# Weight conversion in half steps, one every fourth attention slot, ahead of the row maximum

## The chip, the cores and the metric

The kernel runs on one core of one Trainium2 chip. The metric is the device time of one launch in microseconds (us). Lower is better. The engines are TensorE (PE in the profile; its weight loads are PEld), VectorE (DVE), ScalarE (ACT), GpSimd (POOL) and SyncE (SP), which here only issues transfers. Each takes its instructions in the order in which they stand in its queue; PE may load weights ahead.

## The reference

```python
def _attn_ref(q, k, v, centroids):          # q, k, v: 2 x 8 x 768 x 64, centroids: 8 x 16 x 64
    q_assign = np.argmax(np.einsum('bhsd,hcd->bhsc', q_n, c_n), axis=-1)   # q_n, k_n, c_n: normalized rows
    k_assign = np.argmax(np.einsum('bhsd,hcd->bhsc', k_n, c_n), axis=-1)
    mask = q_assign[:, :, :, None] == k_assign[:, :, None, :]
    scores = np.where(mask, scale * np.matmul(q, k.transpose(0, 1, 3, 2)), -1e9)
    attn = softmax(scores)
    return np.matmul(attn, v)

x = attn_out.transpose(0, 2, 1, 3).reshape(1536, 512)
h = x @ moe_w_in;  x = (h * np.cos(h)) @ moe_w_out        # 512 -> 2048 -> 512, first mixture
h = x @ moe2_w_in; g = blend(h)                           # second mixture: 0, (h+1)^2/4 or h
return g @ moe2_w_out
```

The four weight matrices come as 64-bit floats, which the chip's engines don't multiply.

## The kernel before

**Attention.** The 16 heads are done in 8 pairs of heads, and each pair in 24 slots (one `run_slot` each), 192 slots in all. A slot transposes one 384-column block of the softmax numerator (`p_transpose`: three PE transposes `pt`, an ACT copy `phi`, a DVE remainder `plo`), computes half a score tile (`scores`, two matmuls into `s`) and multiplies earlier blocks with v (`p_v`, into `o`). Every second slot has a row maximum (`row_max`, line 484, DVE, result `nm`) and the exponential that needs it (`row_exp`, ACT). `later(n, f)` puts work n slots ahead. On slots 18 to 179 the order on PE, ACT, DVE and POOL is the order in which the code is written; SP's order and the rest are a scheduler's.

**The next pair's preparation** (`prep_pair`) goes along, a piece a slot: transposes of q and k, their split into two parts `th` and `tl` on POOL (lines 301, 302), the cluster masks, `vv` (lines 439, 440), and copies of `th`, `tl` into the stacked operands `st` by SP transfers (line 315). There are three buffers for `st`. The copies into the second head of pair 5 can start only when the scores of pair 4's first head, the last of which stands in slot 99, have read the buffer. For pairs 1, 3 and 5 `th` and `tl` lie in one buffer of `w0pool`, tag `w_0` (line 282; the trace calls the tile `t`).

**POOL's other work** is the finish of each block of 384 rows: `o_rows` (`xt`, lines 567 and 568), whose sum DVE multiplies with the transposed denominators (`finish`, line 579), and `x_parts` (`xh`, `xl`, lines 584, 585); and the denominators (`den`, `rb`, lines 502, 513).

**Weights.** The 16 tiles of 512x512 come in 32 chunks of 128x1024 64-bit words. `convert_chunk` makes float32 out of one in six steps: ACT takes an absolute value (line 139), DVE clips (141), shifts (143), puts low bits in (146) and the sign and POOL rounds to the first part (149, 155; then the next chunk's load is issued), DVE computes the second part (158). `pump(n)` does the next n steps. `wx` and `wraw`, the chunk and its raw words, have one buffer each. The first tile of weights is written into `w_0`, the buffer that pair 5's `th` and `tl` leave; it can be written first when all their readers are done: the matmuls and all ten copies. In the attention there are 16 steps, one every eighth slot from 69 to 189, behind the slot's row maximum.

**Mixtures.** Per quarter of the hidden width and block of 512 tokens `hidden` makes four groups of 12 matmuls into `h`, each with DVE and ACT work to `gh`, `gl`, and `output` four into `y`. Each group pumps one step. `weight` pumps what is still missing of a tile before its first use. The first two `hidden` calls come ahead of the first `output`.

Of the kernel before, what the change touches and what calls it, by code (L numbers as in the profile page):

```python
# [8 lines left out]
F32 = mybir.dt.float32  # L9
F32R = mybir.dt.float32r  # L10
I32 = mybir.dt.int32
BF16 = mybir.dt.bfloat16
I64 = mybir.dt.int64
AF = mybir.ActivationFunctionType
ALU = mybir.AluOpType
# [3 lines left out]
P = 128  # L19
# [3 lines left out]

HIGH_MIN = 2.0 ** -15
HIGH_MAX = 122876.0
CHUNK = 6
P_BUFS = 6
NDVE = 2
NIDLE = (9, 3, 5, 7, 6)
# [3 lines left out]
def attention_moe_moe(  # L33
# [18 lines left out]
    nc = tc.nc  # L52
# [8 lines left out]
    NQ = DFF // 512  # L61
# [44 lines left out]
    def next_slot():  # L106
        now[0] += 1
        for f, args in due.pop(now[0], ()):
            f(*args)
# [9 lines left out]
    w0pool = ctx.enter_context(tc.tile_pool(name="w0pool", bufs=1))  # L119
    wslot = []  # L120
    wchunks = []
    wraw = {}

    def issue_chunk(n):
        if n >= len(wchunks):
            return
        src, c0, _ = wchunks[n]
        raw = w0pool.tile([P, 2, 512], I64, tag="wraw", bufs=1, name=f"wraw{n}")
        nc.sync.dma_start(raw, src[:, c0:c0 + 2])
        wraw[n] = raw  # L130

    def convert_chunk(n):

        _, c0, w = wchunks[n]
        words = wraw.pop(n).bitcast(I32).rearrange("p c (f t) -> p c f t", t=2)
        low, high = words[:, :, :, 0], words[:, :, :, 1]
        x = w0pool.tile([P, 2, 512], F32, tag="wx", bufs=1, name=f"wx{n}")
        xi = x.bitcast(I32)
        nc.scalar.activation(x, high.bitcast(F32), AF.Abs)  # L139
        yield  # L140
        nc.vector.tensor_scalar(x, x, HIGH_MIN, HIGH_MAX, ALU.max, ALU.min)
        yield
        nc.vector.tensor_scalar(xi, xi, 3, 0x3FFFFFFF,
                                ALU.logical_shift_left, ALU.bitwise_and)
        yield
        nc.vector.scalar_tensor_tensor(xi, low, 29, xi,
                                       ALU.logical_shift_right, ALU.bitwise_or)
        yield
        nc.vector.scalar_tensor_tensor(xi, high, -0x40000000, xi,
                                       ALU.bitwise_and, ALU.bitwise_or)  # L150
        if not wslot:
            wslot.append(w0pool.tile([P, 2, 4, 512], F32R, tag="w_0", name="w_0"))
        t = wslot[w % 4]
        hi, lo = t[:, 0, c0:c0 + 2], t[:, 1, c0:c0 + 2]
        nc.gpsimd.tensor_scalar(hi, x, 1.0, 0.0, ALU.mult, ALU.add)  # L155
        issue_chunk(n + 1)
        yield
        nc.vector.tensor_tensor(lo, x, hi.bitcast(F32), ALU.subtract)
        yield

    for l, (wi, wo) in enumerate(((w1_in, w1_out), (w2_in, w2_out))):
        for qi in range(NQ):
# [6 lines left out]
    def weight_steps():  # L169
        for n in range(len(wchunks)):  # L170
            for _ in convert_chunk(n):
                yield n
# [3 lines left out]
    def pump(n):  # L176

        for _ in range(n):
            at[0] += 1
            next(wsteps, None)  # L180

    at = [0]

    def weight(l, qi, s):
        pump(2 * CHUNK * ((l * NQ + qi) * 2 + s + 1) - at[0])
        t = wslot[((l * NQ + qi) * 2 + s) % len(wslot)]
        return t[:, 0], t[:, 1]


    with ExitStack() as actx:  # L190
# [273 lines left out]
        def scores(n, step):  # L464

            i, h, hf = units[n // HJ]
            j = hf * HJ + n % HJ
            qt, kt = prepped[i][1][h]
            if step == 0:
                ptile[n] = ps_s.tile([P, 2, 512], F32, tag="s", name=f"s{n}")  # L470
            s = ptile[n]
            cols = slice(j * P, (j + 1) * P)
            kc = slice(step * HS, (step + 1) * HS)
            with tc.issue_after(last_po[0]) if n == 0 and step == 0 else ExitStack():
                nc.tensor.matmul(s[:, step, :HS], qt[:, 0, cols], kt[:, 0, kc],  # L475
                                 start=True, stop=False)
            rows = D + C if i else D + 2 * C
            nc.tensor.matmul(s[:, step, :HS], qt[:rows, 1, cols], kt[:rows, 1, kc],  # L478
                             start=False, stop=True)

        def row_max(n):
            nm = ap.tile([P, 1], F32, tag="nm", bufs=8, name=f"nm{n}")
            s = ptile[n]
            nc.vector.tensor_reduce(nm, s[:, :, :HS], AX.XY, ALU.max, negate=True)  # L484
            ptile[n] = (s, nm)

        def row_exp(n):
            s, nm = ptile[n]
# [34 lines left out]
        def p_transpose(u, kt):  # L523
            ps = ps_t.tile([P, HS], F32, tag="t", name=f"pt{u}_{kt}")
            for jj in range(HJ):
                p = ptile[u * HJ + jj].rearrange("p a n -> p (a n)")
                nc.tensor.transpose(ps[:, jj * P:(jj + 1) * P], p[:, kt * P:(kt + 1) * P], ident)  # L527
            hi = ap.tile([P, HS], F32R, tag="phi", bufs=6, name=f"phi{u}_{kt}")
            lo = ap.tile([P, HS], F32R, tag="plo", bufs=6, name=f"plo{u}_{kt}")
            nc.scalar.activation(hi, ps, AF.Copy)  # L530
            pts[(u, kt)] = (hi, lo, ps)

        def p_lo(u, kt):
            hi, lo, ps = pts[(u, kt)]
            nc.vector.tensor_tensor(lo, ps, hi.bitcast(F32), ALU.subtract)  # L535

        def p_v(u, kt):
            i, h, hf = units[u]
            vv = prepped[i][0]
            hi, lo, _ = pts.pop((u, kt))  # L540
            if kt == 0:
                opsum[u] = ps_o.tile([P, HS], F32, tag="o", name=f"o{u}")
            o = opsum[u]
            lhs = vv[:, kt, h * P:(h + 1) * P]
            nc.tensor.matmul(o, lhs, hi, start=(kt == 0), stop=False)  # L545
            nc.tensor.matmul(o, lhs, lo, start=False, stop=(kt == NJ - 1))  # L546
            if kt == NJ - 1:
                later(1, o_parts, u)
# [61 lines left out]
        def run_slot(slot):  # L610
            g = slot + LEAD
            if slot in prep_at:
                preps.append(prep_pair(prep_at[slot]))
            if 0 <= slot < NSLOT:
                p_transpose(slot // NJ, slot % NJ)
            if 0 <= g < NSLOT:
                scores(g // 2, g % 2)
            for u, kt in pv_slots.get(slot, ()):
                p_v(u, kt)
            if slot % 2 == 0:  # L620
                for s in (slot - 1, slot):
                    if 0 <= s < NSLOT:
                        p_lo(s // NJ, s % NJ)
                if 2 <= g < NSLOT + 2:
                    row_exp(g // 2 - 1)
            next_slot()
            if slot == 60:
                issue_chunk(0)
            preps[:] = [p for p in preps if next(p, 0) != 0]
            if slot % 2 == 1 and 0 <= g < NSLOT:  # L630
                row_max(g // 2)
            if 64 <= slot < 192 and slot % 8 == 5:
                pump(1)

# [61 lines left out]
    def mm3(o, lh, ll, rh, rl, first, last):  # L698
        nc.tensor.matmul(o, lh, rh, start=first, stop=False)  # L699
        nc.tensor.matmul(o, lh, rl, start=False, stop=False)  # L700
        nc.tensor.matmul(o, ll, rh, start=False, stop=last)  # L701

    def hidden(l, qi, blk):
        wh, wl = weight(l, qi, 0)
        gh = mp.tile([P, 4, BW], F32R, tag="gh", bufs=2, name=f"gh{l}_{qi}_{blk}")
        gl = mp.tile([P, 4, BW], F32R, tag="gl", bufs=2, name=f"gl{l}_{qi}_{blk}")
        cols = slice(blk * BW, (blk + 1) * BW)
        for f in range(4):
            next_slot()
            ph = ps_h.tile([P, BW], F32, tag="h", name=f"h{l}_{qi}_{blk}_{f}")  # L710
            fs = slice(f * P, (f + 1) * P)
            for c in range(4):
                mm3(ph, wh[:, c, fs], wl[:, c, fs], xh[:, c, cols], xl[:, c, cols],
                    c == 0, c == 3)
            (g_cosine if l == 0 else g_blend)(ph, gh[:, f], gl[:, f], f"{l}_{qi}_{blk}_{f}")
            pump(1)
        return gh, gl

    def output(l, qi, blk, gh, gl):
# [69 lines left out]
```

## Time and profile before

| | |
|---|---|
| runs | 815.85, 817.35, 819.4 us; median 817.35 |
| profiled execution | 820.39 us, of which the span from first to last instruction is 818.6 |
| PE busy | 797.4 us, 97% of the span |
| DVE busy | 629.7 us, 77% |
| ACT busy | 400.3 us, 49% |
| POOL busy | 282.6 us, 35% |
| mean granted TensorE clock | 0.991 of full speed |

Busy time is the time in which an engine works on an instruction; a PE that waits inside a chain of small matmuls can still look busy, since their ends are modelled and overlap. The attention ends near 283 us; what follows is the two mixtures. Times in the views below are from the start of the span. A bracket in a row of a timeline gives the idle time of the engine just before it and whose work ended it.

### The profile page before, as it was taken

The page shows a single profiled execution, that of the slowest core. Times are in us where ns is not written, and L with a number is a line of the kernel's source. Part 1 is how long each engine was busy: PE and PEld are TensorE (multiplying, and loading weights), DVE is VectorE, ACT ScalarE, POOL GpSimd, SP SyncE. Part 2 cuts the span into 40 slices and gives each one's busy share as a digit, 9 for nine tenths or more (in the row PEclk, how much of TensorE's full clock was granted, in tenths as well). Part 3 has the DMA queues.
Part 4 walks back from the last instruction along what each step waited for, and adds up shares of the span by engine and source line. Part 5 has one row for each costly group of instructions (what it writes and reads, how often), then busy time and mean ns, then how long its engine had stood idle before and what let it go on. Part 6 is the DMA issues. An engine that isn't in the chain of part 4 may idle for free.

```text
span 818.6 us, 11285 instructions
## 1 busy us (share of the span) xinstructions
PE 797.4 (97%) x4042; PEld 670.6 (82%) x4042; DVE 629.7 (77%) x957; ACT 400.3 (49%) x762; POOL 282.6 (35%) x425
## 2 busy tenths in 40 slices
PE   8899999999999999999999999999999999999998
PEld 5789988889888877888888888888888888888886
DVE  6878978968899787777977777898876987755552
ACT  3688878767788665443434333323444233222220
POOL 3347558574674532222221112332231122111110
PEclk9999999988999999999999999999999999999999
DMA  7875553565440103213121313112122221000012
GB/s 155 192 147 121 134 126 88 119 154 108 97 89 32 52 2 103 92 63 103 52 91 64 102 52 104 52 54 100 52 70 86 61 86 59 1 1 0 14 50 91
DMA packets 48183, 65.97 MB, mean 81 GB/s; under 512 B 27904, under 2 KB 32640, under 8 KB 48128
## 3 DMA queue, kind: packets, MB, share of 16 engines
q1 hardware_dynamic: 47984, 65.22, 29.5%
q8 instruction: 32, 0.52, 0.3%
q14 instruction: 23, 0.19, 0.1%
q10 hardware_dynamic: 144, 0.03, 0.0%
HBM read 43.02 MB, written 3.15 MB: 56 GB/s over the span
## 4 chain that ended last, share of the span: by engine, by line
PE 76%; DVE 10%; POOL 6%; ACT 4%; issue 2%; DMA 1%; SPq 0%; POOLq 0%; ACTq 0%; DVEq 0%
PE y L699 11%; PE y L700 11%; PE y L701 11%; PE h L701 10%; PE h L699 10%; PE h L700 10%; PE pt L527 4%; DVE plo L535 3%; DVE nm L484 3%; PE s L475 2%; PE s L478 2%; PE o L546 2%; PE o L545 2%; ACT phi L530 1%; PE pd L368 1%
## 5 line engine op out<-in xcount | busy, mean ns | idle before, releaser
L657 POOL TENSOR_SCALAR gh<-g 128x512 fp32r<-128x512 f32 x96 | 71.5, 745 | 278.0 <-DVE g L688 157.4
L699 PE MATMUL h<-xh,w 128*128 128x512 f32 x384 | 151.4, 394 | 0.5 <-DVE g L674 0.5
L700 PE MATMUL h<-xl,w 128*128 128x512 f32 x384 | 151.4, 394 | 0.0
L701 PE MATMUL h<-xh,w 128*128 128x512 f32 x384 | 151.3, 394 | 0.0
L535 DVE TENSOR_TENSOR plo<-pt,phi 128x384 fp32r<-128x384 f32 x192 | 99.6, 547 | 16.6 <-ACT phi L530 15.8
L530 ACT ACTIVATE phi<-pt 128x384 fp32r<-128x384 f32 x192 | 93.2, 494 | 36.2 <-PE pt L527 34.4
L484 DVE TENSOR_REDUCE nm<-s 128x1 f32<-128x768 f32 x96 | 91.0, 948 | 19.8 <-PE s L478 18.8
L527 PE MATMUL pt<-ident,p 128*128 128x128 f32 x576 | 98.5, 279 | 7.8 <-DVE plo L535 5.8
L684 ACT ACTIVATE p<-h,mone 128x512 f32<-128x512 f32 x48 | 33.1, 690 | 130.0 <-DVE m L683 129.6
L493 ACT ACTIVATE p<-s,nm 128x768 f32<-128x768 f32 x96 | 86.6, 902 | 8.8 <-DVE nm L484 7.8
L661 DVE TENSOR_TENSOR gl<-g,gh 128x512 fp32r<-128x512 f32 x96 | 71.6, 746 | 20.0 <-POOL gh L657 15.3
L699 PEld LDWEIGHTS h<-xh,w 128*128 128x128 f32 x384 | 71.9, 187 | 18.4 <-DVE g L674 1.0
L701 PEld LDWEIGHTS h<-xh,w 128*128 128x128 f32 x384 | 71.8, 187 | 17.7
L527 PEld LDWEIGHTS pt<-ident,p 128*128 128x128 f32 x576 | 69.9, 141 | 20.0 <-issue 4.2
L700 PEld LDWEIGHTS h<-xl,w 128*128 128x128 f32 x384 | 71.9, 187 | 17.5
L475 PE MATMUL s<-st,st 128*128 128x384 f32 x192 | 81.6, 425 | 2.5 <-ACT p L493 2.3
L139 ACT ACTIVATE wx<-wraw 128x1024 f32<-128x1024 f32 x32 | 36.5, 1140 | 95.5 <-DMA wraw<-in_moe_w_out_dram 47.7
L699 PE MATMUL y<-gh,w 128*128 128x512 f32 x192 | 74.9, 390 | 1.3 <-POOL w L155 1.3
L700 PE MATMUL y<-gl,w 128*128 128x512 f32 x192 | 74.8, 390 | 0.0
L700 PE MATMUL y<-w,gh 128*128 128x512 f32 x192 | 74.8, 390 | 0.0
L699 PE MATMUL y<-w,gh 128*128 128x512 f32 x192 | 74.7, 389 | 0.0
L738 DVE TENSOR_TENSOR acc<-y,acc 128x512 f32<-128x512 f32 x72 | 49.2, 685 | 33.1 <-PE y L701 33.1
(120 smaller groups left out, 1636.3 us busy)
## 6 DMA issues: line engine op xcount, KB each, us to landing
wraw<-in_moe_w_in_dram SPq DMA_DIRECT2D x16, 1024.0 KB, 5.1
wraw<-in_moe_w_out_dram SPq DMA_DIRECT2D x16, 1024.0 KB, 4.9
st<-t SPq DMA_DIRECT2D x24, 192.0 KB, 4.3
st<-th SPq DMA_DIRECT2D x9, 384.0 KB, 4.0
st<-tl SPq DMA_DIRECT2D x18, 192.0 KB, 4.0
st<-th SPq DMA_DIRECT2D x18, 192.0 KB, 4.3
nat<-in_q_dram SPq DMA_DIRECT2D x8, 384.0 KB, 5.1
nat<-in_k_dram SPq DMA_DIRECT2D x8, 384.0 KB, 5.8
```

The source lines that it names most:

```text
L475: nc.tensor.matmul(s[:, step, :HS], qt[:, 0, cols], kt[:, 0, kc], start=True, stop=False)
L484: nc.vector.tensor_reduce(nm, s[:, :, :HS], AX.XY, ALU.max, negate=True)
L493: nc.scalar.activation(p, s[:, :, :HS], AF.Exp, bias=nm, accum_out=dens[u][:, jj, 0:1])
L527: nc.tensor.transpose(ps[:, jj * P:(jj + 1) * P], p[:, kt * P:(kt + 1) * P], ident)
L530: nc.scalar.activation(hi, ps, AF.Copy)
L535: nc.vector.tensor_tensor(lo, ps, hi.bitcast(F32), ALU.subtract)
L657: nc.gpsimd.tensor_scalar(hi, g, 1.0, 0.0, ALU.mult, ALU.add)
L661: nc.vector.tensor_tensor(lo, g, hi.bitcast(F32), ALU.subtract)
L699: nc.tensor.matmul(o, lh, rh, start=first, stop=False)
L700: nc.tensor.matmul(o, lh, rl, start=False, stop=False)
L701: nc.tensor.matmul(o, ll, rh, start=False, stop=last)
L738: nc.vector.tensor_tensor(a, po, a, ALU.add)
```

## The change

Each of the first three chunks is converted in halves of 128x512: every step is two steps, first on one half, then on the other, twelve in all. In the attention one such step is done every fourth slot (65, 69, ... 189), so that the same 2 2/3 chunks are done there, and it stands ahead of the slot's row maximum, not behind it. In the mixtures a hidden group does two steps until four chunks are made, and `weight` asks for made chunks instead of counting steps.

```diff
-CHUNK = 6
 def convert_chunk(n):
-        nc.scalar.activation(x, high.bitcast(F32), AF.Abs)
-        yield
-        nc.vector.tensor_scalar(x, x, HIGH_MIN, HIGH_MAX, ALU.max, ALU.min)
-        yield
...
+        cuts = [slice(0, 1), slice(1, 2)] if n < 3 else [slice(0, 2)]
+        for c in cuts:
+            nc.scalar.activation(xs[:, c], words[:, c, :, 1].bitcast(F32), AF.Abs)
+            yield
+        for c in cuts:
+            nc.vector.tensor_scalar(xs[:, c], xs[:, c], HIGH_MIN, HIGH_MAX, ALU.max, ALU.min)
+            yield
...
+        for c in cuts:
+            xi = xs[:, c].bitcast(I32)
+            nc.vector.scalar_tensor_tensor(xi, words[:, c, :, 1], -0x40000000, xi,
+                                           ALU.bitwise_and, ALU.bitwise_or)
+            nc.gpsimd.tensor_scalar(t[:, 0, c], xs[:, c], 1.0, 0.0, ALU.mult, ALU.add)
+            if c == cuts[-1]:
+                issue_chunk(n + 1)
+            yield
+        for c in cuts:
+            nc.vector.tensor_tensor(t[:, 1, c], xs[:, c], t[:, 0, c].bitcast(F32), ALU.subtract)
+            if c == cuts[-1]:
+                made[0] = n + 1
+            yield
...
     def weight(l, qi, s):
-        pump(2 * CHUNK * ((l * NQ + qi) * 2 + s + 1) - at[0])
+        while made[0] < 2 * ((l * NQ + qi) * 2 + s + 1):
+            pump(1)
...
             preps[:] = [p for p in preps if next(p, 0) != 0]
+            if 64 <= slot < 192 and slot % 4 == 1:
+                pump(1)
             if slot % 2 == 1 and 0 <= g < NSLOT:
                 row_max(g // 2)
-            if 64 <= slot < 192 and slot % 8 == 5:
-                pump(1)
...
-            pump(1)
+            pump(1 if made[0] > 3 else 2)
```

The first place is POOL's queue at slots 96 to 103, the end of pair 3 and the preparation of pair 6; `w` is the first tile of weights, `wx` the first chunk, and a bracket names the queues and engines for which a row waits. Before:

```order
L513 TENSOR_SCALAR rb_1_2157<-den_2185 128x3x64 [waits DVE_49]
L584 TENSOR_SCALAR xh<-xt_3_0_2410 128x384 [waits DVE_49]
L585 TENSOR_TENSOR xl<-xt_3_0_2410,xh 128x384 [waits Pool_49]
...
L568 TENSOR_TENSOR xt_3_1_2471<-xt_3_1_2471,xt_3_1_2518 128x384 [waits Pool_49]
...
L440 TENSOR_TENSOR vv_2526<-natv_2019,vv_2526 128x6x64 [waits Pool_49]
L155 TENSOR_SCALAR w_2550<-wx_1865 128x1024 [waits DMAHW4_49,DMAHW3_49,DMAHW5_49,DMAHW2_49,DMAHW6_49,DMAHW1_49,DMAHW7_49,DMAHW0_49,DVE_49]
L301 TENSOR_SCALAR th_2607<-t_6_0_0_2617 128x384 [waits Activation_49]
```

And now:

```order
L522 TENSOR_SCALAR rb_1_2160<-den_2188 128x3x64 [waits DVE_49]
L162 TENSOR_SCALAR w_2452<-wx_1798 128x512 [waits DMAHW3_49,DMAHW4_49,DMAHW2_49,DMAHW5_49,DMAHW1_49,DMAHW6_49,DMAHW0_49,DMAHW7_49,DVE_49,PE_49]
L593 TENSOR_SCALAR xh<-xt_3_0_2414 128x384 [waits DVE_49]
L594 TENSOR_TENSOR xl<-xt_3_0_2414,xh 128x384 [waits Pool_49]
...
L577 TENSOR_TENSOR xt_3_1_2478<-xt_3_1_2478,xt_3_1_2525 128x384 [waits Pool_49]
...
L449 TENSOR_TENSOR vv_2533<-natv_2021,vv_2533 128x6x64 [waits Pool_49]
L162 TENSOR_SCALAR w_2452<-wx_1798 128x512 [waits DVE_49]
L310 TENSOR_SCALAR th_2613<-t_6_0_0_2623 128x384 [waits Activation_49]
```

The first write of `w`, with its wait for all eight transfer queues, has moved up from behind `vv` to ahead of `xh`; the half that stays behind `vv` waits for DVE alone.

The second place is DVE's queue at slots 100 to 109 of the same stretch (`plo` as above; `xt_3_1` is the product of line 579, which reads POOL's sum). Before:

```order
L484 TENSOR_REDUCE nm_2547<-s_2492 128x1 [waits PE_49]
L149 SCALAR_TENSOR_TENSOR wx_1865<-wraw_1676,wx_1865 128x1024
...
L535 TENSOR_TENSOR plo_2_2589<-pt_2_2584,phi_2_2588 128x384 [waits DVE_49,Activation_49]
L579 TENSOR_TENSOR xt_3_1_2518<-xt_3_1_2471,r_1_2600 128x384 [waits PE_49,Pool_49]
L484 TENSOR_REDUCE nm_2636<-s_2591 128x1 [waits PE_49]
```

And now:

```order
L160 SCALAR_TENSOR_TENSOR wx_1798<-wraw_1676,wx_1798 128x512
L493 TENSOR_REDUCE nm_2558<-s_2499 128x1 [waits PE_49]
...
L544 TENSOR_TENSOR plo_2_2595<-pt_2_2590,phi_2_2594 128x384 [waits DVE_49,Activation_49]
L588 TENSOR_TENSOR xt_3_1_2525<-xt_3_1_2478,r_1_2606 128x384 [waits PE_49,Pool_49]
L167 TENSOR_TENSOR w_2452<-wx_1798,w_2452 128x512 [waits DMAHW4_49,DMAHW5_49,DMAHW3_49,DMAHW6_49,DMAHW2_49,DMAHW7_49,DMAHW1_49,DMAHW0_49]
L493 TENSOR_REDUCE nm_2643<-s_2597 128x1 [waits PE_49]
```

The last full-width step that put the sign in is a half ahead of the row maximum, and the first half of the second part stands ahead of the row maximum of slot 105, four slots earlier than the whole did.

## Rows read from the trace of the kernel before

**Rows 1.** Busy time by stretch: stretch, us, then each engine's busy time (instructions), clock.
```profile
340.00:700.00 360.00, 360.00 (x1566) 292.90 (x1565) 292.92 (x382) 135.78 (x209) 87.27 (x101) 1.00 0.22 74
```

**Rows 2.** Timeline of DVE: the row maximum of slot 17 of five pairs.
```profile
82.95 0.96 DVE L484 TENSOR_REDUCE nm<-s 128x1 f32<-128x768 f32 x1 [0.73 <-PE s L478]
...
114.37 0.96 DVE L484 TENSOR_REDUCE nm<-s 128x1 f32<-128x768 f32 x1 [0.71 <-PE s L478]
...
146.84 0.96 DVE L484 TENSOR_REDUCE nm<-s 128x1 f32<-128x768 f32 x1 [0.73 <-PE s L478]
...
183.75 0.96 DVE L484 TENSOR_REDUCE nm<-s 128x1 f32<-128x768 f32 x1 [2.73 <-PE s L478]
...
218.27 0.96 DVE L484 TENSOR_REDUCE nm<-s 128x1 f32<-128x768 f32 x1 [0.71 <-PE s L478]
```

**Rows 3.** The chain that ended last, 126 to 143 us: start, us, what.
```profile
126.52 0.55 DVE xt L579
...
127.15 0.77 POOL xh L584
...
139.90 1.02 POOL t L302
...
142.56 0.52 PE pt L527 x3
```

**Rows 4.** Busy time by stretch, ahead of that chain's POOL part.
```profile
128.00:132.00 4.00, 4.00 (x30) 3.85 (x29) 4.00 (x9) 3.51 (x9) 3.67 (x5) 1.00 0.89 185
```

**Rows 5.** Timeline of POOL, slots 96 to 104.
```profile
157.76 0.35 POOL L513 TENSOR_SCALAR rb<-den 128x192 f32<-128x192 f32 x1
160.31 0.76 POOL L584 TENSOR_SCALAR xh<-xt 128x384 fp32r<-128x384 f32 x1 [2.20 <-DVE xt L579]
...
162.25 2.68 POOL L567 TENSOR_SCALAR xt<-xt 64x384 f32<-64x384 f32 x3
165.01 1.01 POOL L568 TENSOR_TENSOR xt<-xt,xt 128x384 f32<-128x384 f32 x1
```

**Rows 6.** Timeline of SP: the five copies into pair 5's second head.
```profile
160.36 4.36 SPq L315 DMA_DIRECT2D st<-t  x5
```

**Rows 7.** Busy time by stretch: the last two columns are DMA's busy share and GB/s.
```profile
166.00:167.00 1.00, 0.74 (x6) 0.49 (x6) 1.00 (x3) 0.83 (x2) 0.84 (x4) 1.00 0.94 203
167.00:168.00 1.00, 1.00 (x8) 0.86 (x9) 0.74 (x2) 1.00 (x4) 0.92 (x2) 1.00 0.17 39
```

**Rows 8.** Timeline of DVE: the product that reads POOL's sum.
```profile
167.21 0.54 DVE L579 TENSOR_TENSOR xt<-xt,r 128x384 f32<-128x384 f32 x1
```

**Rows 9.** The chunk's tile: steps by line, ns min/median/max, first and last start.
```profile
L139 ACT ACTIVATE wx<-wraw x32: 1116/1138/1179, 120.4 to 694.7; 128x1024 f32<-128x1024 f32 x32
L141 DVE TENSOR_SCALAR wx<-wx x32: 676/695/1106, 130.2 to 695.8; 128x1024 f32<-128x1024 f32 x32
...
L146 DVE SCALAR_TENSOR_TENSOR wx<-wraw,wx x32: 1212/1220/1396, 153.3 to 697.8; 128x1024 int32<-128x1024 int32 x32
...
L155 POOL TENSOR_SCALAR w<-wx x32: 1045/1054/1429, 169.9 to 700.4; 128x1024 fp32r<-128x1024 f32 x32
```

**Rows 10.** Timeline: operations of half that width in the mixtures.
```profile
299.26 0.67 DVE L674 SCALAR_TENSOR_TENSOR g<-r,h 128x512 f32<-128x512 f32 x1
...
312.11 0.62 POOL L657 TENSOR_SCALAR gh<-g 128x512 fp32r<-128x512 f32 x1 [2.35 <-DVE g L674]
```

**Rows 11.** Timeline of POOL: the copies of line 567 a pair without steps.
```profile
97.05 1.69 POOL L567 TENSOR_SCALAR xt<-xt 64x384 f32<-64x384 f32 x3
```

**Rows 12.** Busy time by stretch: the column of 1.00 to 0.50 is TensorE's granted clock.
```profile
172.00:176.00 4.00, 2.98 (x20) 2.30 (x18) 2.34 (x4) 2.08 (x5) 3.75 (x6) 1.00 0.34 92
176.00:180.00 4.00, 3.52 (x23) 3.44 (x24) 3.14 (x6) 3.15 (x9) 3.75 (x6) 0.86 0.70 184
180.00:184.00 4.00, 4.00 (x17) 4.00 (x17) 1.27 (x4) 1.28 (x3) 0.91 (x3) 0.50 1.10 273
```

**Rows 13.** Timeline of PE at the mixtures' begin.
```profile
309.22 0.50 PE L699 MATMUL y<-gh,w 128*128 128x512 f32 x1 [1.26 <-POOL w L155]
```

More of the change, by code (lines that the diff above doesn't have):

```diff
@@ L121, in attention_moe_moe @@
     wchunks = []
+    made = [0]
     wraw = {}
@@ L135, in convert_chunk @@
         words = wraw.pop(n).bitcast(I32).rearrange("p c (f t) -> p c f t", t=2)
-        low, high = words[:, :, :, 0], words[:, :, :, 1]
-        x = w0pool.tile([P, 2, 512], F32, tag="wx", bufs=1, name=f"wx{n}")
-        xi = x.bitcast(I32)
-        nc.scalar.activation(x, high.bitcast(F32), AF.Abs)
-        yield
-        nc.vector.tensor_scalar(x, x, HIGH_MIN, HIGH_MAX, ALU.max, ALU.min)
-        yield
-        nc.vector.tensor_scalar(xi, xi, 3, 0x3FFFFFFF,
-                                ALU.logical_shift_left, ALU.bitwise_and)
@@ L145, in convert_chunk @@
[L145 to L150, printed above, removed]
+        xs = w0pool.tile([P, 2, 512], F32, tag="wx", bufs=1, name=f"wx{n}")
+        cuts = [slice(0, 1), slice(1, 2)] if n < 3 else [slice(0, 2)]
+        for c in cuts:
+            nc.scalar.activation(xs[:, c], words[:, c, :, 1].bitcast(F32), AF.Abs)
+            yield
@@ new lines, in convert_chunk @@
+        for c in cuts:
[3 more added lines that the diff above has]
+            xi = xs[:, c].bitcast(I32)
+            nc.vector.tensor_scalar(xi, xi, 3, 0x3FFFFFFF,
+                                    ALU.logical_shift_left, ALU.bitwise_and)
+            yield
+        for c in cuts:
+            xi = xs[:, c].bitcast(I32)
+            nc.vector.scalar_tensor_tensor(xi, words[:, c, :, 0], 29, xi,
+                                           ALU.logical_shift_right, ALU.bitwise_or)
+            yield
@@ L151, in convert_chunk @@
         if not wslot:
             wslot.append(w0pool.tile([P, 2, 4, 512], F32R, tag="w_0", name="w_0"))
[L153 to L159, printed above, removed]
+        t = wslot[w % 4][:, :, c0:c0 + 2]
+        for c in cuts:
+            xi = xs[:, c].bitcast(I32)
+            nc.vector.scalar_tensor_tensor(xi, words[:, c, :, 1], -0x40000000, xi,
[3 more added lines that the diff above has]
+                issue_chunk(n + 1)
+            yield
@@ L161, in attention_moe_moe @@
+        for c in cuts:
+            nc.vector.tensor_tensor(t[:, 1, c], xs[:, c], t[:, 0, c].bitcast(F32), ALU.subtract)
+            if c == cuts[-1]:
+                made[0] = n + 1
+            yield
     for l, (wi, wo) in enumerate(((w1_in, w1_out), (w2_in, w2_out))):
@@ L178, in pump @@
         for _ in range(n):
-            at[0] += 1
             next(wsteps, None)
-    at = [0]
     def weight(l, qi, s):
-        pump(2 * CHUNK * ((l * NQ + qi) * 2 + s + 1) - at[0])
+        while made[0] < 2 * ((l * NQ + qi) * 2 + s + 1):
+            pump(1)
         t = wslot[((l * NQ + qi) * 2 + s) % len(wslot)]
```

## The prediction

> **What bounds the kernel now.** I read the busy times by stretch first. From 340 to 700 us PE is busy 360.00 of 360 [rows 1]: in the mixtures nothing that DVE, ACT or POOL does earlier can save time. All that the change can move lies before, in the attention and the first groups of the mixtures.
>
> There I took the row maximum of slot 17 of each pair as a clock of the slots [rows 2]. The pair before any step takes 114.37 - 82.95 = 31.42 us. The pairs with steps take 32.47, 36.91 and 34.52 us, so 1.05, 5.49 and 3.10 us more. This 9.6 us, and some in the last pair, is what halved and moved steps can win at most.
>
> The chain of work says what a pair is made of. Through the slots from 21 to about 3 of the next pair it is DVE back to back; then it leaves DVE at the product of line 579 (126.52), runs on POOL alone from xh at 127.15 to the split of the next pair's q and k at 139.90, and returns over ACT to PE at 142.56 [rows 3]. In the DVE part DVE is busy 4.00 of 4 us [rows 4]: a step there costs its whole time. In the POOL part, some 14 us, what counts is what delays POOL. Then comes PE's part, around slot 17, where DVE waits 0.71 to 0.73 us for the scores [rows 2]: a step up to that length is free.
>
> **The first half on POOL.** POOL's first write of the weights goes into the buffer that pair 5's th and tl leave, and so waits for the last copy out of it. Before, it stood behind vv, when the copies had landed, and POOL did not wait. Now its first half stands right behind the rb that ends at 157.76 + 0.35 = 158.1 [rows 5]. The last five copies are issued from 160.36 on and take 4.36 us to issue [rows 6], since they wait for the scores of slot 99, which the change doesn't bring forward. The transfers are busy 0.94 of the us from 166 and 0.17 of the next [rows 7], so the last byte lands near 167.2. POOL then stands from 158.1 to 167.3, of which 2.2 us were idle before.
>
> Queued behind it on POOL are xh, xl, three copies and the sum of line 568, den, rb, vv and the next th and tl. A half takes 0.62 us, by POOL's row of that width [rows 10]. So xh starts at 168.0 instead of 160.31, 7.7 us late. Something is given back: before, the sign step ran beside the three copies of line 567 and made them 2.68 us [rows 5] against 1.69 in a pair without steps [rows 11]; now it falls into POOL's wait. The sum of line 568 then ends 6.7 us late, at 172.7 instead of 166.0 [rows 5]. DVE's product of line 579, at 167.21 before [rows 8], waits for it. DVE stands 5.5 us, and behind the product, in its queue, the row maximum and the plo of the following slots; without plo PE runs out of its three transpose buffers and stands too.
>
> Behind that, the second half of w is 0.43 us shorter than the whole (1.05 [rows 9] against 0.62), and the first half of the second part now runs beside POOL's vv. The whole sign step took 1.22 us [rows 9] and stretched POOL by 0.99, so 0.23 less than its length; a half of 0.67 [rows 10] by this stretches it by 0.44. The two cancel. I take **+6.5 us**; bounds 5.5 (only DVE's own stand counts) and 7.7 (nothing is given back).
>
> The Trainium skill, "SBUF — State Buffer", section "Who interferes with whom", says that DVE with two SBUF inputs and GpSimd lock each other out for the whole instruction. By that the half would cost 0.67 and the sum would be 0.2 higher. The rows show the stretch 0.23 us below the length, so I go by the rows.
>
> **The halves on DVE and ACT.** A half of DVE's 1.22 us steps is 0.67 [rows 10], so 0.12 us is added each time. Per chunk: the low-bits step cost 1.22 in DVE's full part; now its first half (slot 17 of the pair) lies in the 0.73 us wait and is free, its second costs 0.67. But the sign step, earlier hidden beside POOL's chain, has its first half in the full part, 0.67. The clip, 0.70 [rows 9], likewise, has one half in the full part, between 0.35 (half of it) and 0.47 (with the 0.12), and less beside POOL. ACT's 1.14 us [rows 9] cost most of a half there, and now one half goes into the wide slot 17. So about +0.1, +0.1 and -0.5: -0.3 us for each of two chunks. In the last pair there is no preparation and DVE has small gaps in each slot, which halves use twice; there and at the attention's end I take -0.8. Together **-1.4**. Bounds: +1.8, if nothing is hidden and only the 15 added DVE operations at 0.12 count; -4, most of the 1.05 + 3.10 us of the pairs without the clock's fall.
>
> SP's load of v moves behind the mask copies and the weight load; its reader comes a pair, 31 us [rows 2], later: nothing.
>
> **The mixtures' begin.** PE waits there once for the fourth chunk, 1.26 us [rows 13]. With two steps a group POOL rounds that chunk several DVE operations earlier. In exchange the g of the first block fall behind two of the conversion's 1.22 us steps, which may let a group of h wait a little. **-1.1**; bounds -1.3 and +1.
>
> **The clock.** TensorE's granted clock is 1.00 (2.4 GHz) through this part, except that it falls to 0.50 (1.2 GHz) behind the stretch in which PE was busy 2.98 of 4 us. In the three stretches from 172 on it reads 1.00, 0.86, 0.50 [rows 12]; the two after them repeat 0.50 and 0.86. That is 1.1 + 4 + 4 + 1.1 = 10.2 us at half speed. If PE bounds all of it, that costs 5.1 us; the row maximum at 183.75 had waited 2.73 us for scores instead of 0.7 [rows 2], so 2.0 by then; I take 4.0. After the change PE stands some 4 us at a stretch near 170, so I expect the fall again, a few us earlier. But then it covers slots in which POOL is late anyway and PE has time: 2.5, bounds 0 and 5.1. Difference **-1.5** (-4 to +1).
>
> **The sum.** 820.39 + 6.5 - 1.4 - 1.1 - 1.5 = 822.9 against the profiled execution, which itself is 3.0 above the median and 1.0 above the highest run. I take the fall of the clock, which a run may have or miss, as the main part of the spread of the runs, and the fall as regular after the change. So the profiled execution is the base, less half a us: **822.5 us**. That is 0.6% above the median of 817.35; a measurement of this kernel can tell about 0.5%, 4.1 us, from no change, so the edges are 813.3 and 821.4.
>
> **The rivals.**
> - *The wait is not there* (other side). If the copies have landed when POOL reaches the first half, +6.5 becomes about -0.4, from the shorter POOL row. Then 820.4 - 0.4 - 1.4 - 1.1 is 817.5 with the clock's fall and 813.5 without. It decides at one point: whether the last copy lands before 158.1. Against it: before, the first of the five was not even issued until 160.36 [rows 6]. For it: nothing in the rows but that the whole w never waited. 0.08.
> - *The wait is there, and more is won back.* The halves save 3 us instead of 1.4 and the clock stays up or falls briefly: 820.4 + 6 - 3 - 1.1 - 3.5 = 818.8. For it speak the 3.10 us of the pair from 183.75, in which the second chunk has no such wait; against it that two DVE halves a chunk now stand in the full part. 0.26.
> - *The clock stays down longer*, since PE, at half speed, cannot catch up with POOL's chain: +1 instead of -1.5, and no gain at the mixtures: 826. 0.10.
> - *The halves cost.* All 15 added operations fall in DVE's full part: +1.8 instead of -1.4, 826. The Trainium skill, "Advanced Engine Details and Errata", section "The Read-Write Bubble", speaks for this: it says that the latency between instructions on VectorE and ScalarE isn't hidden and advises wide tiles. The rows bear it out only in the 0.12 us an operation, of which part lies in DVE's waits. 0.06.
> - *Forecast*, 820 to 825: 0.50.
>
> **How the numbers follow.** Slower by over 0.5% are both rivals at 826 and about four fifths of the forecast: 0.56. Faster is the first rival without the clock's fall, about half of it, and a tenth of the second: 0.07. The rest, 0.37, is within 0.5%. The range goes from 816.5, in the second rival, to 827.
>
> **What would show it.** On POOL, an idle of about 9 us ahead of the first w half with a transfer as releaser, and the sum of line 568 some 6 us later; on DVE, a wait of about 5.5 us for POOL ahead of the product; a pair from 146.5 of about 41 us in the row maxima, with half clock in it; the pair before a little under 32.47, that after nearer 33; no wait of y for w. The forecast is wrong if POOL's first half starts near 158.2, if DVE's stand is absorbed (the pair stays below 38 us), or if the clock does not fall.

## The result and the profile after

The changed kernel takes 821.92 us (median of 13 runs, 820.12 to 828.37), the kernel before beside it on the same chip 816.26 us (13 runs, 815.63 to 820.13). The ratio is 1.0072, 95% interval 1.0049 to 1.0095: slower by 0.7%, and the interval leaves out no change. The forecast was 822.5 us. The profiled execution of the changed kernel took 820.12 us (span 818.3, mean granted clock 0.996); that of before took 820.39.

So the two profiled executions differ by 0.3 us and the medians by 5.7. Both facts are to be explained: what the change adds, and why one profile beside the other hides it. In the changed kernel the old lines 149, 155, 158 are 160, 162, 167; 484 is 493; 439, 527, 535 are 448, 536, 544; 567, 568, 579, 584 are 576, 577, 588, 593; 315 and 292 are 324 and 301.

POOL's timeline of the changed kernel, slots 96 to 104 (before: [rows 5]); the bracket is the idle time and what ended it:

```profile
167.84 0.62 POOL L162 TENSOR_SCALAR w<-wx 128x512 fp32r<-128x512 f32 x1 [10.72 <-DMA st<-oht]
...
170.10 1.68 POOL L576 TENSOR_SCALAR xt<-xt 64x384 f32<-64x384 f32 x3
171.86 0.99 POOL L577 TENSOR_TENSOR xt<-xt,xt 128x384 f32<-128x384 f32 x1
...
173.53 0.94 POOL L448 TENSOR_SCALAR vv<-natv 128x384 fp32r<-128x384 f32 x1
```

SP's timeline of the same kernel, the last copies out of pair 5's `th` and `tl` (before: [rows 6]) and what follows:

```profile
159.28 4.36 SPq L324 DMA_DIRECT2D st<-t  x5
163.73 5.63 SPq L301 DMA_DIRECT2D st<-oht  x8
```

The view of line 324 in the same stretch gives the five copies' first and last issue and the time from issue to landing:

```profile
L324 SPq DMA_DIRECT2D st<-t x5: 597/852/1231, 159.3 to 162.8; - x5
...
DMA to landing us min/median/max: 3.7/3.9/4.6
```

DVE's timeline of the same kernel, the product behind POOL's sum (before, without a wait: [rows 8]):

```profile
172.88 0.56 DVE L588 TENSOR_TENSOR xt<-xt,r 128x384 f32<-128x384 f32 x1 [7.21 <-POOL xt L577]
173.35 0.74 DVE L167 TENSOR_TENSOR w<-wx,w 128x512 fp32r<-128x512 f32 x1
```

PE's timeline, the transpose that waits for that product in turn:

```profile
173.49 0.90 PE L536 MATMUL pt<-ident,p 128*128 128x128 f32 x3 [4.08 <-DVE xt L588]
```

One reads the loss downwards: the copies are issued at 159.28, POOL stands 10.72 us for them, its sum ends at 172.85, DVE stands 7.21 us, PE 4.08.

The row maximum of slot 17 of each pair, the clock of the slots (before: [rows 2]):

```profile
113.71 0.96 DVE L493 TENSOR_REDUCE nm<-s 128x1 f32<-128x768 f32 x1 [0.71 <-PE s L487]
...
145.87 0.96 DVE L493 TENSOR_REDUCE nm<-s 128x1 f32<-128x768 f32 x1
...
188.77 0.96 DVE L493 TENSOR_REDUCE nm<-s 128x1 f32<-128x768 f32 x1 [0.71 <-PE s L487]
...
220.91 0.96 DVE L493 TENSOR_REDUCE nm<-s 128x1 f32<-128x768 f32 x1
```

The pair from 145.87 takes 42.90 us (before 36.91), the next 32.14 (before 34.52). Two rows have no wait for the scores any more: there a half step fills it.

Busy time by stretch (PE, PEld, DVE, ACT, POOL, then granted clock, DMA share, GB/s) in the changed kernel, around the stand:

```profile
164.00:168.00 4.00, 3.39 (x24) 2.56 (x23) 1.68 (x3) 3.42 (x9) 0.16 (x1) 1.00 0.63 136
166.00:167.00 1.00, 0.97 (x8) 0.62 (x6) 0.00 (x0) 1.00 (x3) 0.00 (x0) 1.00 0.35 79
167.00:168.00 1.00, 0.42 (x4) 0.20 (x3) 0.00 (x0) 0.49 (x1) 0.16 (x1) 1.00 0.18 35
168.00:172.00 4.00, 1.41 (x9) 1.08 (x7) 0.00 (x0) 0.49 (x1) 3.58 (x7) 1.00 0.44 97
172.00:176.00 4.00, 2.51 (x10) 2.19 (x11) 3.12 (x7) 1.00 (x3) 3.75 (x6) 0.66 0.49 194
176.00:180.00 4.00, 1.80 (x10) 1.48 (x9) 1.29 (x2) 1.08 (x3) 3.75 (x7) 0.91 0.36 98
180.00:184.00 4.00, 4.00 (x19) 3.90 (x19) 2.35 (x4) 2.17 (x6) 3.75 (x6) 0.57 0.53 121
```

The same view at the mixtures' begin and in the mixtures:

```profile
300.00:320.00 20.00, 20.00 (x87) 15.99 (x86) 17.89 (x23) 9.69 (x17) 8.55 (x8) 1.00 0.16 53
340.00:700.00 360.00, 360.00 (x1565) 292.90 (x1565) 292.77 (x383) 135.55 (x209) 84.82 (x101) 1.00 0.22 74
```

From 164 to 168 POOL is busy for 0.16 us; from 168 to 180 it is the busiest engine, with 3.58 to 3.75 of 4, and the chain of work, followed back from 192 us, stays on POOL from 167.84 to 179.29 and then goes over ACT to PE. TensorE's clock falls twice for a short time, together 4 x (0.34 + 0.09 + 0.43) / 0.5 = 6.9 us at half speed, against 10.2 in the profiled execution before [rows 12]. At 300 to 320 PE is now busy throughout: the wait of [rows 13] is gone. The mixtures after that are unchanged [rows 1].

### The profile page after: what moved, and what is told of

It reads as the page before. It is cut to its first block, busy times and chain, and to the rows that moved or that the text cites. A ratio compares the mean times of both kernels' runs of the same rounds, so it can differ in the third digit from the quotient of the medians.

```text
span 818.3 us, 11309 instructions
## 1 busy us (share of the span) xinstructions
PE 795.6 (97%) x4041; PEld 668.1 (82%) x4042; DVE 632.2 (77%) x972; ACT 399.9 (49%) x765; POOL 279.6 (34%) x428
## 4 chain that ended last, share of the span: by engine, by line
PE 78%; DVE 9%; POOL 7%; ACT 3%; issue 2%; DMA 0%; POOLq 0%; SPq 0%; DVEq 0%; ACTq 0%
PE y L709 11%; PE y L710 11%; PE y L708 11%; PE h L708 11%; PE h L710 10%; PE h L709 10%; PE pt L536 4%; DVE plo L544 3%; DVE nm L493 3%; PE s L484 2%; PE s L487 2%; PE o L554 2%; PE o L555 2%; POOL xl L594 1%; ACT phi L539 1%
## 5 line engine op out<-in xcount | busy, mean ns | idle before, releaser
L140 ACT ACTIVATE wx<-wraw 128x1024 f32<-128x1024 f32 (+1 forms) x35 | 37.0, 1058 | 97.7 <-DMA wraw<-in_moe_w_out_dram 48.2
L709 PE MATMUL y<-w,gh 128*128 128x512 f32 x192 | 74.8, 390 | 0.0
L710 PE MATMUL y<-gh,w 128*128 128x512 f32 x192 | 74.8, 390 | 0.0
L708 PE MATMUL y<-gh,w 128*128 128x512 f32 x192 | 74.8, 389 | 0.0
```

## The experiments

Two theories. **W**: POOL's first half of w waits for the copies out of the buffer, stands at the head of POOL's queue, and that is the loss. **H**: the halves, or their place ahead of the row maximum, cost. **C**, besides: the fall of TensorE's clock behind the stand is a part of the loss. Each ratio is to the kernel before on the same chip, beside it.

| kernel | median us (runs) | lowest | ratio to before, 95% |
|---|---|---|---|
| before | 816.26 (13) | 815.63 | |
| changed | 821.92 (13) | 820.12 | 1.0049 to 1.0095 |
| e1 changed, other buffer | 812.46 (12) | 812.11 | 0.9932 to 0.9987 |
| e2 changed, one late round | 818.30 (12) | 815.67 | 0.9989 to 1.0027 |
| e3 before, round moved ahead | 826.16 (6) | 825.87 | 1.0078 to 1.0131 |
| e4 changed, one step a group | 826.17 (6) | 822.92 | 1.0065 to 1.0130 |
| e5 before, other buffer | 815.96 (12) | 815.52 | 0.9987 to 1.0019 |
| e6 e1, one step a group | 814.07 (12) | 813.01 | 0.9963 to 1.0003 |
| e7 e1, behind the row maximum | 813.76 (12) | 812.36 | 0.9943 to 0.9973 |
| e8 e5, two steps a group | 816.39 (12) | 814.69 | 0.9976 to 1.0007 |
| e9 changed, PE filled once | 823.90 (8) | 820.17 | 1.0057 to 1.0122 |
| e10 changed, PE filled twice | 825.40 (6) | 820.72 | 1.0052 to 1.0112 |
| e11 changed, mask copies back | 822.65 (9) | 820.19 | 1.0053 to 1.0105 |

**e1: the wait taken away.**

```diff
-            if i in (1, 3, 5):
+            if i in (1, 3):
                 t2 = w0pool.tile([P, 2, 2, S], F32R, tag="w_0", name=f"t2_{i}")
```

> The changed kernel with one digit changed: pair 5's th and tl take the attention pool's own th and tl buffers (as pairs 0, 2 and 4 do) and no longer the buffer of the first weight tile, so POOL's first half of w has no copy of pair 5 to wait for; the order of all instructions stays. Theory W (that wait is the loss): POOL does not stand ahead of the half, DVE's product starts near 167 again, the third pair of row maxima comes from 42.9 to 35 to 37 us, and the time from 821.9 to 813.5 to 816. Theory H (halving the steps, or putting them ahead of the row maximum, is the loss): the wait goes but the time stays at 819 to 822.

812.46 us. POOL's timeline of this kernel:

```profile
157.49 0.62 POOL L162 TENSOR_SCALAR w<-wx 128x512 fp32r<-128x512 f32 x1
...
161.59 2.01 POOL L576 TENSOR_SCALAR xt<-xt 64x384 f32<-64x384 f32 x3
163.68 1.02 POOL L577 TENSOR_TENSOR xt<-xt,xt 128x384 f32<-128x384 f32 x1
```

DVE's timeline of the same kernel, the product among the row maxima of slot 17 of four pairs and the attention's last:

```profile
51.17 0.96 DVE L493 TENSOR_REDUCE nm<-s 128x1 f32<-128x768 f32 x1 [1.01 <-PE s L487]
...
146.28 0.96 DVE L493 TENSOR_REDUCE nm<-s 128x1 f32<-128x768 f32 x1
...
166.15 0.54 DVE L588 TENSOR_TENSOR xt<-xt,r 128x384 f32<-128x384 f32 x1
...
180.66 0.96 DVE L493 TENSOR_REDUCE nm<-s 128x1 f32<-128x768 f32 x1 [0.71 <-PE s L487]
...
213.11 0.96 DVE L493 TENSOR_REDUCE nm<-s 128x1 f32<-128x768 f32 x1
...
266.51 0.96 DVE L493 TENSOR_REDUCE nm<-s 128x1 f32<-128x768 f32 x1
```

The half starts right behind `rb`, the product does not wait, and the pair takes 180.66 - 146.28 = 34.38 us against 42.90. All other pairs agree with the changed kernel's to about 0.3 us (the next one 32.45 against 32.14). So the wait costs **8.5 us** in its pair, and 8.0 of them stay in the whole time: the lowest runs are 820.12 and 812.11. W holds, H falls: the halves are faster than the kernel before once the wait is gone, by 0.4% (0.13% to 0.68%). The time came out below the 813.5 to 816 expected. The order of the instructions did not stay quite as it was: on SP's queue, which is a scheduler's, the load of v now goes ahead of the mask copies. e11 tests that order by itself.

**e5: the control.** The same edit in the kernel before.

> The kernel before with pair 5's th and tl in the attention pool's own buffers, nothing else: the control for the other buffer. There POOL's round at slot 101 had no wait, so theory W expects no change: 815.4 to 817.5 as the kernel before. If the other buffer itself gains something (earlier weights, other DMA waits), the time falls by the same amount as it did under the changed kernel beyond the wait, to 812 to 814.

815.96 us, no change: the other buffer gains nothing of its own. Its profiled execution has TensorE's clock at 1.00 through the pair after 146, which the one of before had not, and so gives what the rows of before should be read against. The same row maxima on DVE's timeline:

```profile
146.25 0.96 DVE L484 TENSOR_REDUCE nm<-s 128x1 f32<-128x768 f32 x1 [0.71 <-PE s L478]
...
181.01 0.96 DVE L484 TENSOR_REDUCE nm<-s 128x1 f32<-128x768 f32 x1 [0.72 <-PE s L478]
...
213.44 0.96 DVE L484 TENSOR_REDUCE nm<-s 128x1 f32<-128x768 f32 x1 [0.70 <-PE s L478]
...
268.83 0.95 DVE L484 TENSOR_REDUCE nm<-s 128x1 f32<-128x768 f32 x1
```

Pairs of 34.76 and 32.43 us, where [rows 2] have 36.91 and 34.52: the fall of the clock cost the profiled execution of before 2.15 + 2.09 = 4.2 us.

**e3: the wait alone, without halves.**

```diff
-            if 64 <= slot < 192 and slot % 8 == 5:
+            if 64 <= slot < 192 and (slot == 97 if 97 <= slot < 105 else slot % 8 == 5):
```

> The kernel before with only one step moved: the first chunk's sign step with its whole round on POOL goes from slot 101 to slot 97; whole steps, every eighth slot and one step a group elsewhere as before. Theory W: POOL waits some 9 us ahead of it, the third pair becomes longer by about 6 us, and the time goes from 816.3 to 821 to 825. Theory H: no halves here, so within 1 us of the kernel before, 815.5 to 817.5.

826.16 us, above what W expected. The step still stands behind the row maximum. POOL's timeline:

```profile
170.66 1.04 POOL L155 TENSOR_SCALAR w<-wx 128x1024 fp32r<-128x1024 f32 x1 [12.87 <-DMA st<-oht]
```

SP's timeline of the same kernel, ahead of that:

```profile
159.70 0.38 SPq L129 DMA_DIRECT2D wraw<-in_moe_w_in_dram  x1
161.19 5.49 SPq L315 DMA_DIRECT2D st<-t  x5
```

The sign step, moved ahead, frees `wraw`, so the next chunk's 1024 KB are issued ahead of the five copies and move beside them; these then take 6.0 us to land instead of 4.0. POOL waits 12.87 us, DVE's product 8.57, and the pair takes 44.78 us, 10.0 more than e5's, with 10.2 us at half clock in it. W holds with the halves left out. The price is higher than in the changed kernel; how much of that is the later landing and how much the longer fall of the clock, this run does not tell apart.

**e2: POOL's round whole and late.**

```diff
-            nc.gpsimd.tensor_scalar(t[:, 0, c], xs[:, c], 1.0, 0.0, ALU.mult, ALU.add)
             if c == cuts[-1]:
+                nc.gpsimd.tensor_scalar(t[:, 0], xs, 1.0, 0.0, ALU.mult, ALU.add)
                 issue_chunk(n + 1)
```

> The changed kernel, but POOL's two half rounds of a chunk are one whole instruction, issued at the second sign step (slot 101 of the first chunk) instead of halves at slots 97 and 101. Theory W: POOL reaches it behind xh, xl, the three copies, the sum and vv, when the copies out of the buffer have landed; no wait, and 814 to 816.5. Theory H: 819 to 822. Between them: if POOL now waits a little there because it arrives some us earlier than in the kernel before, 816.5 to 819.

815.67 us in the profiled execution, 818.30 median: between the two. The wait for the copies is gone, but the next step, four slots later, now finds the round not done, in two chunks. DVE's timeline of this kernel, the second chunk:

```profile
235.93 0.98 DVE L167 TENSOR_TENSOR w<-wx,w 128x512 fp32r<-128x512 f32 x1 [2.92 <-POOL w L163]
```

DVE waits 2.9 us each time (2.90 at 169.17 in the first chunk). The first costs nothing that the pairs show (34.58 us against e1's 34.38); the pair with the second takes 33.46 against 29.52, with 3.4 us of half clock in it. A round that comes late for its reader costs too, though less here than one that comes early for its buffer.

**e4 and e6: the mixtures' part undone**, in the changed kernel and in e1.

```diff
-            pump(1 if made[0] > 3 else 2)
+            pump(1)
```

> The changed kernel without its last part: one step a group at the mixtures' begin, as in the kernel before. If the two steps a group are worth what the prediction says, the wait of y for w (1.26 us) is back on PE and the time goes from 821.9 to about 823. If they are worth nothing, it stays at 821.9; since the changed kernel's own runs spread from 820.1 to 828.4, the trace has to decide: PE busy 20.00 of 20 us between 300 and 320 us in the changed kernel, 18.7 if the wait is back.

> The kernel with the other buffer (812.5 us) and one step a group at the mixtures' begin. If the two steps are worth what PE's wait of y for w costs: 813.5 to 814, and PE busy 18.7 of 20 us around 310 us. If nothing: 812.5.

e4's median, 826.17, is no measure of the step: its profiled execution lost 47.45 - 42.90 us in the pair from 146 and 34.75 - 32.14 in the next to a long fall of the clock (from 172.8 to 200.1), far ahead of the mixtures. Two of its six runs, 822.92 and 823.21, lie near the changed kernel's 821.9. Its trace shows the wait of y for w back on PE, 0.73 us ahead of 318.92. PE is busy 18.75 of the 20 us from 300, as expected, but the rest of what it lacks there, 0.52 us, is a wait of h for DVE that the changed kernel has as well, earlier, at 295.01. PE's timeline in e6 shows the same wait:

```profile
308.53 0.50 PE L708 MATMUL y<-gh,w 128*128 128x512 f32 x1 [0.73 <-POOL w L162]
```

e6 gives the size: its five lowest runs lie at 813.01 to 813.55, e1's at 812.11 to 812.34, so the two steps a group are worth **0.9 to 1.2 us**. The wait of y for w that they remove is 0.7 us with halves (e4, e6) and 1.3 with whole steps (e5).

**e7 and e8: place and halves apart.** In e7 the half steps of e1 stand behind the row maximum; e8 is e5 with two steps a group.

```diff
-            if 64 <= slot < 192 and slot % 4 == 1:
-                pump(1)
             if slot % 2 == 1 and 0 <= g < NSLOT:
                 row_max(g // 2)
+            if 64 <= slot < 192 and slot % 4 == 1:
+                pump(1)
```
```diff
-            pump(1)
+            pump(1 if at[0] >= 4 * CHUNK else 2)
```

> The kernel with the other buffer (812.5 us), but each half step stands behind the row maximum of its slot, as the steps did before. If being ahead of the row maximum is worth something, because PE's part of slot 17 lets DVE run a half while it waits for the scores, the time rises by 0.5 to 3 us, and the rows of DVE show longer waits of the row maximum for the scores; by my sum the order within a slot was worth nothing of its own: 812 to 813.

> The kernel before with the other buffer and two steps a group: whole steps every eighth slot, behind the row maximum. Against the kernel with the other buffer (812.5 us) it is the halves and their place together. By my sum these are worth 1.4 us, so 814 against 812.5; if the halves cost (15 added operations of 0.12 us), 811; if they win more, by keeping TensorE's clock up, 815 to 817, with a half-clock stretch behind pair 5 in the trace.

DVE's timeline of e7, the row maximum of slot 17 of the first pair and the attention's last:

```profile
51.45 0.96 DVE L493 TENSOR_REDUCE nm<-s 128x1 f32<-128x768 f32 x1 [1.01 <-PE s L487]
...
267.07 0.95 DVE L493 TENSOR_REDUCE nm<-s 128x1 f32<-128x768 f32 x1
```

The same two in e8:

```profile
51.27 0.96 DVE L484 TENSOR_REDUCE nm<-s 128x1 f32<-128x768 f32 x1 [1.00 <-PE s L478]
...
269.14 0.95 DVE L484 TENSOR_REDUCE nm<-s 128x1 f32<-128x768 f32 x1
```

e7 takes 215.62 us between the two, e1 215.34; the lowest runs are 812.36 and 812.11. So the place is worth 0.3 us in the shortest runs. The medians are 1.3 us apart: six runs of e7 lie at 813.6 to 814.3, where e1 has one, at clocks of 0.996 to 0.998; what makes them longer is not shown. e8, whole steps, takes 217.87 us for the same stretch, and 814.69 in its lowest run. Halves are worth 217.87 - 215.62 = **2.3 us**.

**e9 and e10: PE kept busy through the stand.** POOL's wait stays; zeros are multiplied into score columns that the next matmul overwrites. e9 has the first of the two insertions, e10 both.

```diff
+            if slot == 107:
+                for _ in range(24):
+                    nc.tensor.matmul(ptile[g // 2][:, 1, :HS], idle[:, :P], idle[:, :HS],
+                                     start=True, stop=True)
             if 0 <= slot < NSLOT:
                 p_transpose(slot // NJ, slot % NJ)
...
             for u, kt in pv_slots.get(slot, ()):
                 p_v(u, kt)
+            if slot == 108:
...
```

> The changed kernel with 24 matmuls of zeros, 128x384, on PE ahead of the transpose that stood 4.08 us for DVE's product (slot 107); they write columns of the scores that the next real matmul overwrites, so nothing computed changes. By the duration of such a matmul (0.16 to 0.18 us) they fill about those 4 us. POOL's wait stays. Theory C (PE's stand lets the clock fall, and the fall is part of the loss and all of the changed kernel's spread from 820 to 828): TensorE's clock stays up behind 172 us, the third pair goes from 42.9 to 41 to 42, and the runs gather at 817.5 to 819.5. Theory W alone (only the wait costs, PE had time to spare at half speed): the third pair stays at 42.5 to 43 and the time at 819.5 to 821, whether the clock falls or not. If the zeros themselves delay PE: above 821.

> The kernel with the 24 matmuls of zeros (820.2 us in its profiled execution, 823.9 median) and 16 more of them ahead of PE's second stand, 2.63 us before the transpose of pair 6's q and k in slot 108, behind which the clock still fell (180.60 to 184.01 us, with PE busy 4.00 of 4 from 180 to 184). Nothing computed changes. If that fall and longer ones of its kind in other runs are what the changed kernel loses beyond POOL's wait, the clock stays up from 172 to 190 us, the third pair comes to 41 to 42 us, the runs gather at 818.5 to 820, and none is above 822. If the fall costs nothing here, the third pair stays at 42.9 and the profiled time at 820.2. If the spread has another cause, runs at 825 to 829 remain.

e9's profiled execution took 820.17 us. PE's timeline of it, the zeros and a transpose behind the second fall:

```profile
169.28 4.08 PE L625 MATMUL s<-idle 128*128 128x384 bf16 x24
...
184.54 0.52 PE L536 MATMUL pt<-ident,p 128*128 128x128 f32 x3
```

Busy time by stretch in the same execution:

```profile
168.00:172.00 4.00, 4.00 (x26) 2.80 (x26) 0.00 (x0) 0.49 (x1) 3.58 (x7) 1.00 0.16 29
172.00:176.00 4.00, 3.07 (x20) 1.83 (x17) 3.07 (x7) 0.95 (x3) 3.75 (x6) 1.00 0.78 262
```

DVE's timeline in the same execution, the row maximum of slot 17:

```profile
145.91 0.96 DVE L493 TENSOR_REDUCE nm<-s 128x1 f32<-128x768 f32 x1
...
188.81 0.96 DVE L493 TENSOR_REDUCE nm<-s 128x1 f32<-128x768 f32 x1 [0.71 <-PE s L487]
```

The first fall is gone (1.00 where the changed kernel has 0.66), and the pair still takes 188.81 - 145.91 = 42.90 us, to the hundredth. So that fall cost nothing: POOL was the path. The second fall is still there in e9 (0.57 from 180 to 184). In e10 both are filled: two of its runs had a mean granted clock of 1.000 and took 820.72 and 820.91, no less than the changed kernel's five best runs (820.12 to 820.33).

The other four runs of e10 took 824.50 to 827.06. Its profiled execution is one of them, with the clock at 1.00 until 185.95. PE's timeline of it has the transpose that stands at 184.54 in e9:

```profile
185.47 0.52 PE L536 MATMUL pt<-ident,p 128*128 128x128 f32 x3 [0.21 <-DVE plo L544]
```

DVE's timeline in the same execution, the row maxima of slot 17:

```profile
146.82 0.96 DVE L493 TENSOR_REDUCE nm<-s 128x1 f32<-128x768 f32 x1
...
192.82 0.96 DVE L493 TENSOR_REDUCE nm<-s 128x1 f32<-128x768 f32 x1 [2.73 <-PE s L487]
...
227.80 0.96 DVE L493 TENSOR_REDUCE nm<-s 128x1 f32<-128x768 f32 x1
```

Busy time by stretch in the same execution:

```profile
184.00:188.00 4.00, 3.39 (x20) 3.31 (x21) 2.43 (x4) 2.75 (x7) 3.42 (x6) 0.74 0.67 134
188.00:192.00 4.00, 4.00 (x18) 4.00 (x17) 1.10 (x4) 1.37 (x3) 0.55 (x2) 0.50 0.98 195
```

Counted from the pair's row maximum, that transpose starts after 185.47 - 146.82 = 38.65 us, and in e9, behind the second fall, after 184.54 - 145.91 = 38.63. So the second fall cost nothing either, and C falls for the short falls.

From 185.95 on the clock is at half, until 199.6. PE, busy 4.00 of 4 from 188, is then the path, while POOL has little or nothing to do. The two pairs take 46.00 and 34.98 us: 5.9 us more than with the short falls. A long fall is thus what lengthens this run, and the mean clocks of the changed kernel's upper runs (0.980 to 0.993) speak for the same there. Keeping PE busy in both stands did not prevent such falls: that part of my theory fell.

**e11: the mask copies put back** behind the load of v on SP's queue, as before.

```diff
...
-                        copy(dst, oht[r0:r0 + C])
+                        with tc.issue_after(ins(vload[0])) if i == 5 else ExitStack():
+                            copy(dst, oht[r0:r0 + C])
```

> The changed kernel with one order on SP's queue put back: the eight mask copies of pair 5 stand behind the load of v again (as in the kernel before), and so cannot run right behind the five copies of pair 5's th and tl. In the changed kernel they are issued at 163.73, and the trace names one of them, not one of the five, as what releases POOL's first half at 167.84; the transfers' bulk is over by about 166.3. If the mask copies' company makes the wait longer, the half starts at 166 to 166.6, DVE's product waits 5.7 us instead of 7.2, the third pair comes to 41.2 to 41.7, and the time falls by 1.3 us, to 818.5 to 820 in its best runs. If the half waits for the five alone, it starts at 167.6 to 168 and the time stays at 820.1.

No change in time (best run 820.19). POOL's timeline:

```profile
168.17 0.62 POOL L162 TENSOR_SCALAR w<-wx 128x512 fp32r<-128x512 f32 x1 [10.83 <-DMA st<-t]
```

SP's timeline, the five copies:

```profile
159.50 4.36 SPq L325 DMA_DIRECT2D st<-t  x5
```

From the first issue to POOL's half it is 8.67 us here and 8.56 in the changed kernel. SP issues the mask copies at 177.94 here, long after the half has started, so the half does not wait for them; the name `st<-oht` in the changed kernel's bracket is another transfer that landed at about that time. The five copies still had company: the next chunk's load moved up into the mask copies' place, at 163.97.

## Why the prediction came out

**The number.** 822.5 against 821.92, by the mechanism foretold, but that it lies so near is partly luck. Three terms were off: the wait cost more, the halves won more, and the short falls of the clock cost nothing. With the measured terms the sum is 820.0, which is close to the shortest runs (820.1); the median is moved up from there by long falls of the clock that the forecast did not have.

**The first half on POOL: right in kind, too small.** Foretold +6.5 with bounds 5.5 and 7.7; measured 8.5 in the pair and 8.0 in the whole time (e1), above the upper bound either way. The step that was mis-sized is the landing of the last copy. I read it as near 167.2 from the end of DMA's busy time in [rows 7], and let POOL start 6.9 us after the first issue at 160.36. The runs give 8.56 and 8.67 us (changed kernel, e11). The last of the five is issued 3.5 us after the first and lands 4.6 us later, near 167.4, and POOL starts at 167.84. DMA's busy share falls ahead of that: it is 0.35 in the microsecond from 166 and 0.18 in the next, and the small mask copies, issued from 163.73 on, are part of it. By the same 8.56 us the copies of the kernel before let go near 168.9 (an estimate); its whole w started at 169.9 [rows 9], so it missed the wait by about a us only.

The rest is the time given back. I took a whole us for the three copies, 2.68 against 1.69; beside a half they take 2.01 (e1), so the wait gives back only 0.3 there. The exchange rate held: I foretold 6.5 us for a sum 6.7 late. Now POOL's sum ends at 172.85, and e1's at 164.70, which is 0.41 earlier on the changed kernel's clock of slots (146.28 against 145.87). That is 8.15 + 0.41 = 8.6 us, the 8.5 of the pair. DVE's own stand, 7.21 us, is less than that, since behind it POOL stays the path.

The stretch of POOL beside the second part is as foretold: `vv` takes 0.94 instead of 0.51 us (173.53) beside a DVE operation of 0.74 (173.35 to 174.09), 0.43 against the 0.44 taken. By the Trainium skill, "SBUF — State Buffer", section "SBUF: two separate sides", of a VectorE operation with two SBUF inputs and a GpSimd operation that reads SBUF the one that starts first holds the shared port pair for its whole instruction. By that `vv` would have had to wait until 174.09 and to end at 174.60. It ends at 174.47, so the rows show nearly, not all of, the lock.

**The halves: 2.3 instead of 1.4.** By pairs, e1 against e5 (with the place in it): 0.38 and 0.0 us in the two pairs with preparation (foretold 0.3 for each chunk), then from the row maximum near 213 to the last one 268.83 - 213.44 = 55.39 against 266.51 - 213.11 = 53.40, so 2.0, where 0.8 was foretold: more of the gain lies in the last slots than I gave it. The rival in which the halves cost (15 operations at 0.12 us) is out.

**The mixtures' begin: as foretold**, 0.9 to 1.2 (e6 against e1), and 815.52 - 814.69 = 0.8 between the lowest runs of e5 and e8, for 1.1.

**The clock: right for before, wrong for after.** The fall in the profiled execution before cost 4.2 us (e5), foretold 4.0. The short falls after were given 2.5 and cost nothing (e9, e10). I took a regular fall after the change as part of the time; in truth the runs split: five of 13 at 820.1 to 820.3, eight from 821.9 to 828.4 at mean clocks of 0.980 to 0.993.

**The sum, made anew.** 815.5 (lowest run of e5) + 8.0 - 2.3 - 0.3 (the place) - 0.9 = 820.0, against 820.1 to 820.3 in the five shortest runs. The median, 821.92, lies among the other eight. The two profiled executions looked alike because the one before held a fall of 4.2 us and the one after two that cost nothing.

**What stays open.** Why the clock stays at half for so much longer in one run than in the next of the same kernel. From the mean clocks and spans of the changed kernel's runs one can estimate 6.5 us at half in the shortest (0.996) and 33 in one of the longest (0.980). e1 has long falls too, in three of 12 runs (817.61 to 821.74, mean clocks 0.985 to 0.992), so it is not the wait alone; e9 and e10 show that filling PE's two stands is not enough.

The version that the experiments point to is e1: the change with pair 5's `th` and `tl` in another buffer, 812.46 us, faster than both kernels.

## What to carry to other kernels

When an instruction is moved ahead on an in-order engine, ask of each buffer that it writes who still reads it, and add up the readers' whole way: the wait for their issue, the issuing itself, and the time to landing of the last, not the moment at which DMA's busy share falls. What stands behind the wait is then late by all of it as long as that engine is the path; here one buffer's name was worth 8 us, more than halves, place and two steps a group together. Before two single profiles are compared, see whether a fall of the clock lies in one of them, and take the medians' side.

## What the runs showed of the hardware

- Five copies of 192 to 384 KB, issued over 4.36 us, landed 3.7 to 4.6 us after their issue (changed kernel); the POOL instruction that waits for them started about 0.5 us behind the last landing, 8.56 us after the first issue. Behind a load of 1024 KB they took 6.0 us to land instead of 4.0 (e3).
- A short fall of TensorE's clock cost nothing where POOL was the path (42.90 us for the pair with the first fall and, in e9, without it). A long one, 13.65 us at half, cost 5.9 us where PE was busy 4.00 of 4 (e10).
- In e10's profiled execution the clock fell at 185.95, after five stretches of 4 us from 164 to 184 in which PE had been busy 3.42 to 3.95.
